# Beginning the second group's 48-point stage inside the first sort, with tile tables by partition

## The chip, the cores and the metric

The kernel runs on one core of a Trainium2 chip. The metric is the device time of one execution in microseconds, as the median of several runs. TensorE (PE in the profile) multiplies matrices into PSUM, VectorE (DVE) and ScalarE (ACT) work on SBUF and PSUM, GpSimd (POOL) works on SBUF and issues the scatters, SyncE (SP) issues most loads and stores.

## The reference

Two layers follow each other. The first is a long convolution: every one of 8 batches of 5696 tokens with 128 channels is convolved with a filter by a real FFT of twice the length. The second is a mixture of 8 experts: each token goes to the expert with the largest logit, through two matrices with a ReLU between, and is scaled by its probability.

```python
Xf = np.fft.rfft(x, n=2 * S, axis=1); Hf = np.fft.rfft(h, n=2 * S, axis=0)
y = np.fft.irfft(Xf * Hf[None], n=2 * S, axis=1)[:, :S]
logits = y.reshape(B * S, D) @ w_gate
expert_idx = np.argmax(logits, axis=1)          # probs = softmax(logits)
out[mask_e] = probs_e * (np.maximum(y[mask_e] @ w1[e], 0) @ w2[e])
```

## The kernel before

The transform is split into 120 points along one axis and 48 along the other. The 8 batches form three groups of 2, 3 and 3. Each group passes three phases. `phase_a` is the 120-point DFT: it reads x, and its results go to a DRAM buffer U. `phase_b` is the 48-point stage: 120 items for the second and third group, each with a forward product (tile xp, read from a load uq of U), a multiplication by the filter (`product`: three VectorE operations into zt and xs, with the filter's tile hh), a sum of the two (`combine`, zt), an inverse product (vp), and a copy (`save`) that goes to DRAM as V. An item's product runs one step after its xp, its sum two, its vp four, its copy five steps after. For the sums `ALONE` says from which item on GpSimd takes them instead of VectorE; for the splits of the third group (`cut`) `FIRST` says so. `phase_c` is the 120-point inverse, the gate and the sort: `score` and `route` find each token's expert, `rank` counts on VectorE where each token goes in a DRAM buffer SR that is sorted by expert (pi), and `sort` scatters the rows there from GpSimd, six a rank, with a small memset between two (`REST`, into a spare `mi` or `hh` buffer). In the first group `lift` brings the 48-point results from the SBUF tile `big` by transposes.

After the sort of a group `tables` computes on one partition, with some thirty-five small VectorE operations, which row and expert each tile of 256 sorted tokens has. `fill` pads SR behind the last token of each expert after the last sort, from ScalarE's DMA queue, with the tile `dummy` as its source. `experts` then takes tile after tile: load xr, weights wb (loaded only where the expert changes), transposes mx, first layer mh, ReLU hs, second layer ma, and a scatter to the output.

The order of all instructions is written out by hand: every phase is a generator that yields a planned cost, and `run` interleaves them by cost over share. Four calls of `run` follow each other: the first group's DFT; its 48-point stage beside the preparation of the weights; its sort beside the second group's DFT (`SHARES[1]`) and the rest of the preparation; and at last the experts beside `rest`, in which the second and third group pass their 48-point stage and sort. There the experts wait until `begin` marks a part as ready. That is when the next group's 48-point stage has been given `HEAD` ns of planned cost; two pieces of `tables` are emitted after each of its steps. Between two of these calls the SBUF pools close and new ones open. SP works off its loads and stores in the order in which they were emitted.

Of the kernel before, what the change touches and what calls it, by code (L numbers as in the profile page):

```python
# [40 lines left out]
FIRST = 12  # L41
# [7 lines left out]
SHARES = (0.42, 0.195, 0, 0.75, 0.998, 0.42)  # L49
GAP = 5000  # L50
AHEAD = 2
ALONE = (0, 14, 10)
# [9 lines left out]
XR = 19  # L62
PACE = (1800, 2200)
ROOM = 28
REST = (224, 288, 288)
# [6 lines left out]
def conv_moe(ctx: ExitStack, tc: tile.TileContext, I, out, B, S, D, E, F, split):  # L72
# [17 lines left out]
    KEEP = ("wb", "hs")  # L90

    class Space:
# [9 lines left out]
        def tile(self, shape, dt, tag, name, **kw):  # L102
            return (keep if tag in KEEP + ("base", "did") else self.pool).tile(shape, dt, tag=tag, name=name, **kw)

# [94 lines left out]
    jrow = load_const("jrow", [1, total])  # L199
# [241 lines left out]
    def phase_b(gr):  # L441
# [126 lines left out]
        def inverse(n):  # L568
# [4 lines left out]
            vp = ps.tile([P, 512], F32, tag="cx", name=f"vp{g}_{q}_{c}", bufs=4)  # L573
# [141 lines left out]
    def phase_c(pt, guest=None):  # L715
# [75 lines left out]
        def settle(n, k):  # L791
            if k == 0:
                tag, bufs = ("rt", 6) if g else (("hs", 4), ("rt", 3))[n % 2]
# [78 lines left out]
        def rank(n):  # L872
# [46 lines left out]
        for n in range(n_end + 1):  # L919
            for k in range(nsub):  # L920
# [37 lines left out]
    def tables(pt):  # L958
# [3 lines left out]
        cnt = sb.tile([1, E], F32, tag="cnt", name=f"cnt{g}")  # L962
        nc.vector.tensor_tensor(out=cnt, in0=base[0:1, :E], in1=base0[0:1, :E], op=ALU.subtract)
        ci = sb.tile([1, E], I32, tag="ci", name=f"ci{g}")
        nc.vector.tensor_scalar(
            out=ci, in0=cnt, scalar1=float(T - 1 if last else 0), scalar2=None, op0=ALU.add
        )
        nc.vector.tensor_scalar(out=ci, in0=ci, scalar1=SHIFT, scalar2=None, op0=ALU.arith_shift_right)
        yield
        nt = sb.tile([1, E], F32, tag="nt", name=f"nt{g}")  # L970
        nc.vector.tensor_copy(nt, ci)
        prior = state.get("done")
        if prior is not None:
            nc.vector.tensor_tensor(out=nt, in0=nt, in1=prior, op=ALU.subtract)
        end = sb.tile([1, E + 1], F32, tag="end", name=f"end{g}")
        none = E if down else 0
        nc.vector.memset(end[:, none : none + 1], 0.0)
        for k in range(E):
            if k % 4 == 0:
                yield  # L980
# [4 lines left out]
        low, high = slice(0, E), slice(1, E + 1)  # L985
        ahead, upto = (end[:, high], end[:, low]) if down else (end[:, low], end[:, high])
        start = sb.tile([1, E + 1], F32, tag="start", name=f"start{g}")
        nc.vector.memset(start, float(E * CAP))
        here, after = (start[:, high], start[:, low]) if down else (start[:, low], start[:, high])
        if prior is not None:  # L990
            nc.vector.tensor_tensor(out=here, in0=prior, in1=ahead, op=ALU.subtract)
        else:
            nc.vector.tensor_scalar(out=here, in0=ahead, scalar1=-1.0, scalar2=None, op0=ALU.mult)
        nc.vector.scalar_tensor_tensor(
            out=here, in0=here, scalar=float(T), in1=base0[0:1, :E], op0=ALU.mult, op1=ALU.add
        )
        stp = sb.tile([1, E], F32, tag="stp", name=f"stp{g}")
        nc.vector.tensor_tensor(out=stp, in0=after, in1=here, op=ALU.subtract)
        jr = jrow[:, :NT]
        yield  # L1000
        ge = sb.tile([1, E, NT], F32, tag="yt", name=f"ge{g}")
        nc.vector.tensor_tensor(
            out=ge,
            in0=jr.rearrange("p (o j) -> p o j", o=1).broadcast_to([1, E, NT]),
            in1=upto.rearrange("p (e o) -> p e o", o=1).broadcast_to([1, E, NT]),
            op=ALU.is_ge,
        )
        yield
        ej = sb.tile([1, NT], F32, tag="ej", name=f"ej{g}", bufs=1)
        nc.vector.tensor_reduce(out=ej, in_=ge.rearrange("p e j -> p j e"), axis=AX.X, op=ALU.add)  # L1010
        yield
        nc.vector.tensor_tensor(
            out=ge, in0=ge, in1=stp.rearrange("p (e o) -> p e o", o=1).broadcast_to([1, E, NT]), op=ALU.mult
        )
        yield
        r0 = sb.tile([1, NT], F32, tag="r0", name=f"r0{g}", bufs=1)
        nc.vector.tensor_reduce(out=r0, in_=ge.rearrange("p e j -> p j e"), axis=AX.X, op=ALU.add)
        yield
        nc.vector.scalar_tensor_tensor(out=r0, in0=jr, scalar=float(T), in1=r0, op0=ALU.mult, op1=ALU.add)
        nc.vector.tensor_scalar(out=r0, in0=r0, scalar1=start[:, none : none + 1], scalar2=None, op0=ALU.add)  # L1020
        tab = const.tile([1, 3, NT], I32, name=f"tab{g}")
        nc.vector.tensor_scalar(out=tab[:, 0, :], in0=r0, scalar1=float(E * CAP), scalar2=None, op0=ALU.min)
        yield
        nc.vector.tensor_scalar(out=ej, in0=ej, scalar1=float(E - 1), scalar2=None, op0=ALU.min)
# [17 lines left out]
        nc.vector.tensor_tensor(out=tab[:, 2, back:], in0=ej[:, back:], in1=ej[:, : NT - back], op=ALU.not_equal)  # L1042
        yield
        pt.need = const.tile([1, 1], I32, name=f"need{g}")
        nc.vector.tensor_copy(pt.need, end[:, E - none : E - none + 1])
        pt.tab = tab
# [3 lines left out]
        if not last:  # L1050
            did = sb.tile([1, E], F32, tag="did", name=f"did{g}")
# [7 lines left out]
            state["done"] = did  # L1059

# [242 lines left out]
    def chain(*gens):  # L1303
        for x in gens:
            yield from x
# [47 lines left out]
    g0 = groups[0]  # L1353
    with tc.manual_schedule():
# [10 lines left out]
        run((chain(*[gather(pt) for pt in g0.parts]), 1.0), (phase_a(groups[1]), SHARES[1]), (prep, SHARES[5]))  # L1365
# [83 lines left out]
```

## Time and profile before

| what | value |
|---|---|
| median of 3 runs | 2157.73 us (2156.82 to 2159.77) |
| the profiled execution | 2157.51 us |
| its span, first to last instruction | 2155.7 us |
| TensorE busy | 2082.7 us, 97% |
| VectorE, ScalarE, GpSimd busy | 1542.5, 1114.9, 1350.0 us |
| mean granted TensorE clock | 0.976 |

The profile is of one execution. Its page cuts the span into 40 slices of 53.9 us and gives for each the busy tenths of the engines and the granted clock of TensorE. Where TensorE is busy at full clock, a slice shows 9 in both lines. The stretches in which it doesn't are looked at in the trace: windows for sums, events in order of time for who waited for whom, the chain of work that ended last, and groups of instructions by line for the mean time of one.

### The profile page before, as it was taken

What the parts mean: (1) busy time and instruction counts of PE and PEld (TensorE: products, weight loads), DVE (VectorE), ACT (ScalarE), POOL (GpSimd) and SP (SyncE); (2) the same over time, 40 slices, a digit from 0 to 9 for tenths busy, and PEclk for the clock granted to TensorE, in tenths of its full rate; (3) what the DMA queues carried; (4) which work ended last, traced back from release to release, by engine and by line L of the source; (5) the groups of instructions that cost most, each with busy time, mean ns of one, the idle gap of its engine ahead of it and who ended that gap; (6) DMA issues with size and microseconds to landing.
All of it is one profiled execution on the core that took longest, in us unless ns stands there. A gap on an engine that the chain in (4) does not pass through costs nothing.

```text
span 2155.7 us, 47101 instructions
## 1 busy us (share of the span) xinstructions
PE 2082.7 (97%) x14452; PEld 1863.3 (86%) x14452; DVE 1542.5 (72%) x3373; ACT 1114.9 (52%) x2317; POOL 1350.0 (63%) x1569
## 2 busy tenths in 40 slices
PE   9999999799999999989999999999999999999998
PEld 7799777377777889878888888999999999999998
DVE  4698677799997777688888887666665555555554
ACT  5677555143334666534555555555544454444544
POOL 6566388545554388888998775288883444443333
PEclk9999999599999999999999999999999999999999
DMA  8899799999997898868878885656533244343331
GB/s 269 263 289 293 227 297 281 256 237 256 248 267 196 232 276 255 245 168 229 204 205 222 216 203 153 159 132 159 141 103 98 87 132 135 129 133 126 123 121 34
DMA packets 216993, 420.33 MB, mean 195 GB/s; under 512 B 32501, under 2 KB 136235, under 8 KB 216740
## 3 DMA queue, kind: packets, MB, share of 16 engines
q1 hardware_dynamic: 187263, 360.52, 59.7%
q0 software_dynamic: 27072, 55.35, 8.9%
q8 instruction: 117, 1.92, 0.4%
q10 hardware_dynamic: 2405, 1.43, 0.2%
q14 instruction: 136, 1.11, 0.2%
HBM read 582.45 MB, written 154.27 MB: 342 GB/s over the span
## 4 chain that ended last, share of the span: by engine, by line
PE 82%; DMA 9%; DVE 3%; POOL 2%; issue 2%; ACT 1%; SPq 1%; ACTq 0%; POOLq 0%; DVEq 0%
PE mh L167 23%; PE ma L167 22%; PE vp L167 9%; PE xp L167 9%; PE yp L167 5%; PE mx L189 4%; PE pa L167 3%; DMA xt<-x 3%; PE gb L167 2%; DMA wb<-WD 2%; DMA mt<-mq 2%; PE tp L189 1%; PE hp L167 1%; PE lb L189 1%; DMA U<-ut 1%
## 5 line engine op out<-in xcount | busy, mean ns | idle before, releaser
L1173 DVE SCALAR_TENSOR_TENSOR hs<-mh,hs 128x512 fp32r<-128x512 f32 x728 | 501.6, 689 | 387.5 <-ACT hs L1171 381.2
L167 PE MATMUL mh<-xtb,wb 128*128 128x256 f32 x4368 | 706.4, 297 | 23.0 <-DVE hs L1173 5.2
L1171 ACT ACTIVATE hs<-mh 128x512 fp32r<-128x512 f32 x728 | 435.4, 598 | 488.1 <-PE mh L167 475.4
L167 PEld LDWEIGHTS mh<-xtb,wb 128*128 128x128 f32 x4368 | 589.8, 191 | 92.6 <-issue 37.9
L167 PE MATMUL ma<-hs,wb 128*128 128x256 f32 x4368 | 658.3, 287 | 1.7 <-DMA wb<-WD 1.7
L167 PEld LDWEIGHTS ma<-hs,wb 128*128 128x128 f32 x4368 | 574.4, 191 | 2.9 <-DMA wb<-WD 2.7
L665 POOL DMA_INDIRECT SR<-rt,pi x384 | 406.0, 1057 | 196.2 <-issue 58.9
L683 POOL DMA_INDIRECT out<-xr x310 | 305.4, 985 | 354.2 <-ACT hs L1171 172.6
L566 POOL TENSOR_TENSOR zt<-zt,xs 128x384 f32<-128x384 f32 (+1 forms) x276 | 295.8, 1074 | 155.2 <-DVE xs L556 103.9
L603 ACT COPY vt<-vp 96x384 f32<-96x384 f32 x240 | 114.2, 476 | 260.8 <-PE vp L167 256.6
L560 DVE TENSOR_TENSOR xs<-xp,hh 64x384 f32<-64x384 f32 (+1 forms) x360 | 214.8, 597 | 7.8
L167 PE MATMUL vp<-zt,mi 128*96 128x384 f32 x480 | 200.5, 500 | 0.0
L551 DVE TENSOR_TENSOR zt<-xp,hh 128x384 f32<-128x384 f32 (+1 forms) x300 | 173.6, 579 | 28.7 <-PE xp L167 18.4
L167 PE MATMUL xp<-uq,mt 96*128 96x384 f32 (+1 forms) x496 | 177.7, 462 | 8.5 <-DMA uq<-U 5.1
L167 PE MATMUL pa<-xc,fcr 120*120 120x512 f32 x576 | 159.4, 411 | 1.9 <-POOL xc L284 1.0
L556 DVE SCALAR_TENSOR_TENSOR xs<-xp,hh 64x384 f32<-64x384 f32 x240 | 134.3, 560 | 4.2
L167 PE MATMUL yp<-vr,gcr 120*120 120x384 f32 x576 | 119.5, 343 | 7.1 <-ACT ut L317 7.1
L167 PEld LDWEIGHTS vp<-zt,mi 128*96 128x96 f32 x480 | 79.7, 167 | 49.8 <-issue 26.7
L167 PEld LDWEIGHTS pa<-xc,fcr 120*120 120x120 f32 x576 | 99.9, 186 | 25.2 <-DVE rk L884 2.6
L167 PEld LDWEIGHTS xp<-uq,mt 96*128 96x128 f32 x496 | 87.6, 200 | 33.5 <-issue 12.8
L317 DVE COPY ut<-pa 120x512 f32<-120x512 f32 x96 | 65.7, 684 | 68.6 <-PE pa L167 54.7
L749 DVE TENSOR_TENSOR vr<-vq,vr 120x768 fp32r<-120x768 f32 x96 | 91.5, 954 | 31.8 <-ACT vr L748 31.0
(165 smaller groups left out, 2720.9 us busy)
## 6 DMA issues: line engine op xcount, KB each, us to landing
wb<-WD SPq DMA_DIRECT2D x728, 512.0 KB
U<-ut SPq DMA_DIRECT2D x48, 720.0 KB
uq<-U SPq DMA_DIRECT2D x60, 576.0 KB
V<-vt SPq DMA_DIRECT2D x60, 576.0 KB
vq<-V SPq DMA_DIRECT2D x48, 720.0 KB
xt<-x SPq DMA_DIRECT2D x96, 240.0 KB
hh<-HS SPq DMA_DIRECT2D x120, 192.0 KB
xr<-SR SPq DMA_DIRECT2D x155, 130.0 KB
```

Of the source, the lines that this page charges most:

```text
L167: nc.tensor.matmul(to, lhs, rhs, **kw)
L189: nc.tensor.transpose(dst, src, ident[:n, :n])
L551: nc.vector.tensor_tensor(out=zt, in0=x3, in1=hv[:, 0].broadcast_to([P, PK, cb, D]), op=ALU.mult)
L556: nc.vector.scalar_tensor_tensor(out=xs[to, 0], in0=x3[at, 0], scalar=-1.0, in1=him[:, 0], op0=ALU.mult, op1=ALU.mult)
L560: nc.vector.tensor_tensor(out=xs[to], in0=x3[at], in1=him, op=ALU.mult)
L566: eng.tensor_tensor(out=zt, in0=zt, in1=xs, op=ALU.add)
L603: done = nc.scalar.copy(outs_[qb][:, k0 : k0 + PK, c * cw : (c + 1) * cw], banks.pop(n)[:K2, :iw].rearrange("p (q x) -> p q x", q=PK),)
L665: s = nc.gpsimd.indirect_dma_start(out=SR[:, :], out_offset=IndirectOffsetOnAxis(ap=pi[:, b : b + 1], axis=0), in_=rt[:, b, :], in_offset= ...
L683: sc = nc.gpsimd.indirect_dma_start(out=out[:, :], out_offset=IndirectOffsetOnAxis(ap=xr[:, s, D + 1 : D + 2].bitcast(I32), axis=0), in_=x ...
L749: nc.vector.tensor_tensor(out=vr[:, 1], in0=src, in1=vr[:, 0].bitcast(F32), op=ALU.subtract)
L1171: done = nc.scalar.activation(hs[:, 0], hp, AF.Relu)
L1173: done = nc.vector.scalar_tensor_tensor(out=hs[:, 1], in0=hp, scalar=0.0, in1=hs[:, 0].bitcast(F32), op0=ALU.max, op1=ALU.subtract)
```

## The change

The sort of the first group is no longer run to its end beside the second group's DFT. `lifting` runs it until its last transposes from `big` are emitted; then the pools close, and the rest of it (five steps and an end) is run from `rest`: the first loads of the second group's 48-point stage, then the remaining sort steps, with two items of the 48-point stage behind each from the third on (`HEADS`). Then the stage goes on as before, with `HEAD` counted from there. Until the first part is ready, vp takes PSUM banks of tag mh. The tiles of the sort that outlive the pools move to the pool `keep`. The first filter loads take the `hh` buffers in another order, the second of them later. `tables` holds an expert per partition (9 partitions) and takes sums over experts by five small matmuls with a constant `tcol`. The memset between scatters writes `dummy` for all groups, 2 x 112 columns instead of 224 or 288. `SHARES[1]` goes from 0.195 to 0.2, `ALONE` from 14 and 10 to 5 and 8, `FIRST` from 12 to 10.

```diff
-FIRST = 12
+FIRST = 10
...
-SHARES = (0.42, 0.195, 0, 0.75, 0.998, 0.42)
+SHARES = (0.42, 0.2, 0, 0.75, 0.998, 0.42)
...
-ALONE = (0, 14, 10)
+ALONE = (0, 5, 8)
...
+HEADS = 2
...
-REST = (224, 288, 288)
+REST = 112
...
-    KEEP = ("wb", "hs")
+    KEEP = ("wb", "hs", "rt", "yt", "lmax", "ls", "ex", "wm", "oh", "sm", "cum", "rk", "pi", "base", "did")
...
+        def load_h(qb):
+            hhs[qb] = hhbufs[(qb + 2) % 3]
+            for k in range(2):
+                nc.sync.dma_start(hhs[qb][k * HP : k * HP + NB, :QB], HS[:, qb * QB : (qb + 1) * QB])
...
-            if g != 0:
-                hhs[qb] = hhbufs[qb % 3]
-                for k in range(2):
-                    nc.sync.dma_start(hhs[qb][k * HP : k * HP + NB, :QB], HS[:, q : q + QB])
             tiles[qb] = (uq, mi)
+            if g != 0 and (g, qb) != (1, 1):
+                load_h(qb)
...
-            vp = ps.tile([P, 512], F32, tag="cx", name=f"vp{g}_{q}_{c}", bufs=4)
+            tag, bufs = ("mh", 2) if g == 1 and not parts[0].ready else ("cx", 4)
+            vp = ps.tile([P, 512], F32, tag=tag, name=f"vp{g}_{q}_{c}", bufs=bufs)
...
+        if g == 1:
+            yield 0
+            load_h(1)
...
                 if n < nu - QUICK:
-                    idle = hhbufs[2].rearrange("p a b d -> p (a b d)") if g else mibufs[3].rearrange("p a x -> p (a x)")
-                    nc.gpsimd.memset(idle[:, : REST[g]], 0.0)
+                    nc.gpsimd.memset(dummy[:, :, :REST], 0.0)
...
+                if g == 0 and at == total_sub - 3:
+                    state["lifted"] = True
...
-        for k in range(E):
-            if k % 4 == 0:
-                yield
-            e = E - 1 - k if down else k
-            a, b = (e + 1, e) if down else (e, e + 1)
-            nc.vector.tensor_tensor(out=end[:, b : b + 1], in0=end[:, a : a + 1], in1=nt[:, e : e + 1], op=ALU.add)
         yield
...
+        mm(bank[:E1, 0:1], tcol[:, 7 + E1 * down : 7 + E1 + E1 * down], nt, start=True, stop=True)
...
-        ge = sb.tile([1, E, NT], F32, tag="yt", name=f"ge{g}")
-        nc.vector.tensor_tensor(
-            out=ge,
-            in0=jr.rearrange("p (o j) -> p o j", o=1).broadcast_to([1, E, NT]),
...
+        begun, ended, over = col("begun", NT), col("ended", NT), col("over", NT)
+        nc.vector.tensor_scalar(out=begun, in0=jr, scalar1=ahead, scalar2=here, op0=ALU.is_ge, op1=ALU.mult)
+        nc.vector.tensor_scalar(out=ended, in0=jr, scalar1=upto, scalar2=here, op0=ALU.is_ge, op1=ALU.mult)
+        nc.vector.tensor_scalar(out=over, in0=jr, scalar1=upto, scalar2=None, op0=ALU.is_ge)
         yield
...
+        mm(bank[:1, :NT], tcol[:, 5:6], begun, start=True, stop=False)
+        mm(bank[:1, :NT], tcol[:, 6:7], ended, start=False, stop=True)
+        mm(bank[:1, 128 : 128 + NT], tcol[:, 5:6], over, start=True, stop=True)
+        mm(bank[:1, 256:257], nt, tcol[:, 1:2], start=True, stop=True)
...
-            bins = phase_b(gr)
-            for n, cost in enumerate(bins):
-                if guest and n == QN * gr.nch - 12:
+            bins = enumerate(phase_b(gr))
+            if gr.g == 1:
+                next(bins)
+                for n, cost in enumerate(first_sort):
+                    yield cost
+                    if n >= HEADS:
+                        for _ in range(2):
+                            yield next(bins)[1]
+            for n, cost in bins:
+                if guest and n == QN * gr.nch - 12 + (gr.g == 1):
                     guest.start()
...
+    first_sort = gather(g0.parts[0])
+
+    def lifting():
+        while "lifted" not in state:
+            yield next(first_sort)
...
-        run((chain(*[gather(pt) for pt in g0.parts]), 1.0), (phase_a(groups[1]), SHARES[1]), (prep, SHARES[5]))
+        run((lifting(), 1.0), (phase_a(groups[1]), SHARES[1]), (prep, SHARES[5]))
```

## Rows read from the trace of the kernel before

**Rows 1.** the page: TensorE clock in tenths of full speed, 40 slices

```profile
PEclk9999999599999999999999999999999999999999
```

**Rows 2.** windows: busy of PE, PEld, DVE, ACT, POOL; clock, DMA share, GB/s

```profile
400.00:420.00 20.00, 16.95 (x24) 6.03 (x24) 19.05 (x47) 2.37 (x5) 8.82 (x10) 0.50 0.95 263
...
440.00:460.00 20.00, 20.00 (x111) 14.64 (x110) 19.36 (x36) 8.09 (x17) 10.89 (x11) 1.00 0.93 232
```

**Rows 3.** events of 377 to 426 us: start, us, engine, line, operation, idle before

```profile
377.84 0.94 PE L167 MATMUL pa<-xc,fcr 120*120 120x512 f32 x3
...
385.26 1.23 SPq L473 DMA_DIRECT2D uq<-U  x1
...
392.43 0.25 DVE L890 TENSOR_REDUCE pi<-rk 120x6 int32<-120x54 f32 x1
...
394.07 5.46 PE L167 MATMUL xp<-uq,mt 96*128 96x384 f32 x8 [2.72 <-DMA uq<-U]
...
396.15 0.56 DVE L551 TENSOR_TENSOR zt<-xp,hh 128x384 f32<-128x384 f32 x1 [2.35 <-DMA hh<-HS]
...
409.72 1.00 POOL L665 DMA_INDIRECT SR<-rt,pi  x1 [0.30 <-issue]
...
412.27 0.18 DVE L1042 TENSOR_TENSOR tab<-ej 1x36 int32<-1x36 f32 x1
...
413.21 1.99 SPq L1134 DMA_DIRECT2D wb<-WD  x4
...
425.12 1.89 PE L167 MATMUL mh<-xtb,wb 128*128 128x256 f32 x6 [0.46 <-ACT xtb L1155]
```

**Rows 4.** chain that ended last, 300 to 470 us: start, us, engine, tile

```profile
427.01 1.28 PE xp L167 x2
...
432.32 0.65 PE xp L167 x2
```

**Rows 5.** groups by line, 373 to 450 us: busy, mean ns, idle before

```profile
L551 DVE TENSOR_TENSOR zt<-xp,hh 128x384 f32<-128x384 f32 x20 | 11.1, 555 | 3.3 <-DMA hh<-HS 2.4 <-PE xp L167 0.6
...
L566 DVE TENSOR_TENSOR zt<-zt,xs 128x384 f32<-128x384 f32 x14 | 7.8, 559 | 0.4
...
L566 POOL TENSOR_TENSOR zt<-zt,xs 128x384 f32<-128x384 f32 x6 | 6.3, 1054 | 33.7 <-DVE xs L556 33.7
...
L896 POOL MEMSET mi<- 128x224 f32 x19 | 5.9, 309 | 0.0
```

**Rows 6.** windows at the start of the third group's 48-point stage

```profile
950.00:960.00 10.00, 6.68 (x33) 5.11 (x32) 9.58 (x25) 2.82 (x6) 8.23 (x11) 0.83 0.43 101
```

**Rows 7.** events of 953 to 954 us

```profile
953.51 0.36 POOL L896 MEMSET hh<- 128x288 f32 x1
...
953.90 0.78 SPq L480 DMA_DIRECT2D hh<-HS  x2
```

**Rows 8.** VectorE's groups by line, 932 to 985 us

```profile
L1010 DVE TENSOR_REDUCE ej<-ge 1x67 f32<-1x536 f32 x1 | 1.1, 1102 | 0.0
...
L1012 DVE TENSOR_TENSOR ge<-ge,stp 1x536 f32<-1x536 f32 x1 | 0.7, 705 | 0.0
...
L983 DVE TENSOR_TENSOR end<-end,nt 1x1 f32<-1x1 f32 x8 | 1.2, 154 | 0.2
...
L1019 DVE SCALAR_TENSOR_TENSOR r<-c_jrow,r 1x67 f32<-1x67 f32 x1 | 0.2, 216 | 0.0
```

**Rows 9.** events of 1591 to 1612 us, behind the last sort

```profile
1591.89 0.26 DVE L890 TENSOR_REDUCE pi<-rk 120x6 int32<-120x54 f32 x1
...
1600.08 0.39 ACTq L1076 DMA_DIRECT2D SR<-dummy  x1
...
1606.99 0.60 ACT L1171 ACTIVATE hs<-mh 128x512 fp32r<-128x512 f32 x1 [3.74 <-DMA sp_zt<-SR]
...
1608.36 1.52 PE L167 MATMUL mh<-xtb,wb 128*128 128x256 f32 x6 [2.26 <-DVE start L988]
...
1611.36 0.37 POOL L896 MEMSET hh<- 128x288 f32 x1
```

More of the change, by code (lines that the diff above doesn't have):

```diff
@@ L102, in tile @@
         def tile(self, shape, dt, tag, name, **kw):
-            return (keep if tag in KEEP + ("base", "did") else self.pool).tile(shape, dt, tag=tag, name=name, **kw)
+            return (keep if tag in KEEP else self.pool).tile(shape, dt, tag=tag, name=name, **kw)
     sb = Space()
@@ L965, in tables @@
+        cnt = col("cnt")
+        nc.vector.tensor_reduce(out=cnt, in_=diag, axis=AX.X, op=ALU.add)
+        yield
         nc.vector.tensor_scalar(
-            out=ci, in0=cnt, scalar1=float(T - 1 if last else 0), scalar2=None, op0=ALU.add
+            out=cnt, in0=cnt, scalar1=tcol[:, 0:1], scalar2=tcol[:, 1:2], op0=ALU.subtract, op1=ALU.mult
         )
+        ci = col("ci", dt=I32)
+        add = tcol[:, 4:5] if last else tcol[:, 2:3]
+        nc.vector.tensor_scalar(out=ci, in0=cnt, scalar1=add, scalar2=None, op0=ALU.add)
@@ L968, in tables @@
+        yield
         nc.vector.tensor_scalar(out=ci, in0=ci, scalar1=SHIFT, scalar2=None, op0=ALU.arith_shift_right)
[L969 to L970 removed]
+        nt = col("nt")
         nc.vector.tensor_copy(nt, ci)
[L972 removed]
         if prior is not None:
             nc.vector.tensor_tensor(out=nt, in0=nt, in1=prior, op=ALU.subtract)
[L975 to L976 removed]
@@ L987, in tables @@
[L987 to L993, printed above, removed]
-        nc.vector.scalar_tensor_tensor(
-            out=here, in0=here, scalar=float(T), in1=base0[0:1, :E], op0=ALU.mult, op1=ALU.add
-        )
@@ new lines, in tables @@
+        bank = ps.tile([P, 512], F32, tag="cx", name=f"ah{g}", bufs=4)
+        mm(bank[:E1, 0:1], tcol[:, 7 + E1 * down : 7 + E1 + E1 * down], nt, start=True, stop=True)
+        yield
+        ahead, upto, here = col("ahead"), col("upto"), col("here")
+        nc.vector.tensor_copy(ahead, bank[:E1, 0:1])
+        yield
+        nc.vector.tensor_tensor(out=upto, in0=ahead, in1=nt, op=ALU.add)
+        nc.vector.scalar_tensor_tensor(
+            out=here, in0=ahead, scalar=float(-T), in1=at, op0=ALU.mult, op1=ALU.add
@@ L1015, in tables @@
+        mm(bank[:1, 256:257], nt, tcol[:, 1:2], start=True, stop=True)
         yield
         r0 = sb.tile([1, NT], F32, tag="r0", name=f"r0{g}", bufs=1)
-        nc.vector.tensor_reduce(out=r0, in_=ge.rearrange("p e j -> p j e"), axis=AX.X, op=ALU.add)
+        ej = sb.tile([1, NT], F32, tag="ej", name=f"ej{g}", bufs=1)
+        nc.vector.scalar_tensor_tensor(
+            out=r0, in0=jr[0:1], scalar=float(T), in1=bank[:1, :NT], op0=ALU.mult, op1=ALU.add
+        )
+        nc.vector.tensor_scalar(
+            out=ej, in0=bank[:1, 128 : 128 + NT], scalar1=float(E - 1), scalar2=None, op0=ALU.min
+        )
@@ L1018, in tables @@
+        pt.need = const.tile([1, 1], I32, name=f"need{g}")
+        nc.vector.tensor_copy(pt.need, bank[:1, 256:257])
         yield
-        nc.vector.scalar_tensor_tensor(out=r0, in0=jr, scalar=float(T), in1=r0, op0=ALU.mult, op1=ALU.add)
-        nc.vector.tensor_scalar(out=r0, in0=r0, scalar1=start[:, none : none + 1], scalar2=None, op0=ALU.add)
         tab = const.tile([1, 3, NT], I32, name=f"tab{g}")
         nc.vector.tensor_scalar(out=tab[:, 0, :], in0=r0, scalar1=float(E * CAP), scalar2=None, op0=ALU.min)
-        yield
@@ L1049, in tables @@
             nc.vector.tensor_copy(state["left"], ej[:, NT - 1 :])
-        if not last:
-            did = sb.tile([1, E], F32, tag="did", name=f"did{g}")
+            did = sb.tile([E1, 1], F32, tag="did", name=f"did{g}")
             nc.vector.tensor_scalar(
@@ L1059, in tables @@
             state["done"] = did
+            state["at"] = const.tile([E1, 1], F32, name=f"at{g}")
+            nc.vector.scalar_tensor_tensor(
+                out=state["at"], in0=did, scalar=float(T), in1=tcol[:, 3:4], op0=ALU.mult, op1=ALU.add
+            )
     def begin(pt):
@@ L1419 @@
     ltri = (m[:, None] < m[None, :]).astype(f32) - 1
-    jrow = np.arange((B * S - E) // T + E)[None, :]
+    jrow = np.tile(np.arange((B * S - E) // T + E)[None, :], (E + 1, 1))
+    e = np.arange(E + 1)
+    own = (e < E) * 1.0
+    far = (1 << 20) * (1 - own)
+    tcol = np.stack([e * (B * S + T) * own, own, far, e * (B * S + T), (T - 1) * own + far, own * 0 + 1, own * 0 - 1], 1)
+    up = (e[:, None] < e[None, :]) * 1.0
+    dn = ((e[:, None] > e[None, :]) | (e[None, :] == E)) * own[:, None]
+    tcol = np.concatenate([tcol, up, dn], 1)
     ins = {
@@ L1439 @@
         "jrow": jrow.astype(f32),
+        "tcol": tcol.astype(f32),
     }
```

38 lines of the change are left out of this document (11 added, 27 removed).

## The prediction

> **What bounds the kernel now.** I read the clock line of the page first [rows 1]: TensorE is busy nearly throughout, and the one slice at half clock is the eighth, 377 to 431 us, where the first sort ends and the second group's 48-point stage begins. So a gain must come from a stretch where TensorE waits or runs slow. Windows come second [rows 2]: at 400 to 420 us it has 24 matmul instructions at a clock of 0.50, at 440 to 460 us 111 at 1.00 with all 20.00 us busy. Third comes the order of events in that stretch [rows 3]: the last DFT product of the second group at 377.84, the load uq that waits for its result issued at 385.26, the last rank (pi) at 392.43, the first xp at 394.07, its product on VectorE at 396.15 (held by hh), GpSimd's last scatter at 409.72, the tile table at 412.27, the weight loads at 413.21, the first expert matmul mh at 425.12. Two more stretches matter because the edit touches their queues: the start of the third group's 48-point stage at 930 to 980 us [rows 6 to 8] and the pad rows behind the last sort at 1600 to 1620 us [rows 9].
>
> **Part 1: the first window.** Gained: eight more items of the 48-point stage are drawn ahead of the experts (two after each of four sort steps), then eight again as before until HEAD is spent. LULL then lets three more pass. So 19 forward products stand ahead of the first mh, not 11. An item costs TensorE one xp and one vp of the same 384 columns, 0.65 us each at full clock [rows 4], and the window 440 to 460 us, like those after it, has no TensorE time left [rows 2]: 8 x 1.30 = 10.4 us is saved **if the first mh is no later than now**. Break-even: mh 10.4 us later, at 435.5.
>
> Lost: the delay of that mh. What comes sooner is the DFT. Its half steps are planned at 279/0.2 = 1395 instead of 1431, so after 71 of them the last product stands ahead of the sort's step 29, not behind it: some 4.5 us, before 373.5. The order of loads on SP is unchanged, so uq, the first xp and the first product move with it: 380.8, 389.6 and 391.7. What comes later is the sort: now the first two xp stand ahead of its last gate product on TensorE, and the first product stands ahead of rank 14 on VectorE. Rank 15 then stands behind five products and four sums. From 391.7 on VectorE alone has: twelve products of three operations, 0.555 us and two like it (12 x 1.67 = 20.0); the five sums that stay with it (5 x 0.559 = 2.8) [rows 5]; 18 small operations of two ranks and a route, about 0.25 each like pi [rows 3] (4.5); 19 small operations of the table at about 0.2 each like the row of L1019 [rows 8] (3.8). Together 31.1: table at 422.8, instead of 412.4. Behind the table 0.8 us to the weight loads and 11.9 to mh, as now [rows 3]: 435.5, just break-even. But a V store and another set of loads now stand ahead of the weights on SP, on DMA that is 0.95 busy [rows 2]. If they are off the path they cost nothing; if the set takes as long as the first one from issue to use it is 8.8 [rows 3]. I take 2, since V and most of that set are issued while VectorE still works on the table. So mh at 437.5, a delay of 12.4 against 10.4: **+2**. The best end is hh landing 3 us sooner yet, mh at 432.5, **-3**; the worst is the whole 8.8, **+9**. The sums from item 5 on go to GpSimd, behind the scatters. These end at about 415 (rank 15 near 407, after five products, four sums and the 18 small operations; then six at 1.0 and 0.30 each [rows 3]), about when TensorE at half clock asks for the first of them: no term of its own, though 2 us if rank 15 slips by as much.
>
> The Trainium skill ("GPSIMD Engine Reference", 4.1 Engine selection) speaks against that move: an elementwise sum belongs on VectorE, GpSimd takes about twice as long. The trace agrees, 1054 ns against 559 [rows 5]. By the page eleven sums would cost 5.4 us more if GpSimd were last; by the rows it idles 33.7 us before six of them [rows 5], so I price the move by what leaves VectorE.
>
> **Part 2: the third group's start.** From 940 to 970 us VectorE is busy 9.6 of each 10 us and TensorE less than 9; one of the three windows is shown [rows 6]. Here every operation taken off VectorE counts. The old table has two reductions at 1.1 us and two wide operations at 0.7 on one partition [rows 8], 3.6 us; the new one has three comparisons of 67 elements and a few columns in their place, six at about 0.2 like L1019, 1.2 us. The chain of eight one-element sums (1.2 us [rows 8]) becomes a matmul that idle TensorE takes. Two sums (0.56 each) and one cut of the same size go to GpSimd, which by then has ended its sort. Saved: 2.4 + 1.2 + 1.7 = 5.3. Besides, SP's hh load at 953.90 stood behind GpSimd's memset of that buffer (ended 953.87) [rows 7], with weight loads queued behind it; the memset goes to another tile now. VectorE was busy meanwhile, so I add only 0.7. **-6**, from 0 (the two new matmuls that wait for VectorE give it back) to -9.
>
> **Part 3: the pad rows.** The memset between two scatters now writes `dummy`, and `fill` sends `dummy` from ScalarE's queue. So its first DMA must wait for the last memset of the last sort, which GpSimd reaches late. That such a write holds a DMA is what rows 7 show; that a DMA held on ScalarE's queue holds the relus behind it is shown at 1606.99, where a relu waited 3.74 us and TensorE lost 2.26 [rows 9]. Now the first pad DMA leaves at 1600.08 and waits for nothing; the last memset is at 1611.36. Shorter memsets (0.31 instead of 0.37 [rows 5, 9]) help little: from the rank at 1591.9 twelve scatters are still to go, 12 x (1.00 + 0.31) = 15.7 and the gaps between them, so the last memset ends between 1608 and 1611.4; I take 1610. ScalarE stands still for 9.9 us. TensorE has about 1.5 us of slack per held relu (3.74 less 2.26), so it loses some 8.4. After a wait it runs at half clock for a while, as at 427 us [rows 4]: 1 to 3 more. If the wait at 1606.99 falls into the longer one, up to 4 come back. **+9**, from +5 to +12; 0 if nothing holds the DMA.
>
> **Nothing else**: GpSimd's shorter memsets in the other sorts free an engine that is late for nobody until 1600; the kept buffers have the same depths; the table's matmuls of one column are under 1 us per table and fall into stretches where TensorE waits.
>
> **Sum** on the profiled execution, 2157.5 us (0.2 below the median): +2 - 6 + 9 = +5, so 2162.5.
>
> **The rivals.** *The pad DMA holds nothing* (the other side, not slower). Decided at one place: whether the first pad DMA leaves at the time of the last sort's rank or behind the last memset. Then +2 - 6 = -4: 2153.5. Against it: rows 7 show just this kind of wait. *The first window pays.* If TensorE, with vp in banks of its own, is dense enough on the sixteen steps, its clock comes back before the experts start: in the trace it works 17 of 20 us at 0.50 [rows 2], and steps of 2 x 1.28 become 2 x 0.65 [rows 4]. Then the six half-clock us behind the first mh (425 to 432, [rows 4]) cost 3 less, and loads at their early end 5 less: -6 instead of +2, total 2154.5. The Trainium skill ("TensorE: Matmul & The Clock Gate", What's actually happening) has it so: throttled is the default and activity releases it. Rows alone speak for and against: VectorE's 31 us, not TensorE, set the table, so a faster clock gives nothing ahead of mh. *Both of these*: 2145.5. *The interleave starves*: the loads queue fully ahead of the weights, +9 instead of +2: 2169.5. *The change doesn't do what it says*: uq still lands only at 394 and eight items wait in front of the sort's end; that is 4.5 us more in part 1, 2167.
>
> **Chances.** Forecast (2159 to 2166) 0.45; pad holds nothing 0.15; first window pays 0.18; both 0.07; starved or not sooner 0.15. 0.2%, 4.3 us, is about what a measurement of this kernel can tell from no change. Of the forecast's 0.45, 0.33 lie above 2162 and 0.12 within; with the starved cases slower gets 0.48. The two middle rivals lie near the lower bound: 0.16 of them within, so same 0.28, and faster 0.24 with "both". The range reaches to 2149 and 2172 and leaves out most of "both" and the worst ends.
>
> **What would show it.** Right: uq issued near 381, a rank near 395 behind a product, mh near 437 with some 19 xp ahead of it; VectorE under 9.6 of 10 near 950, hh not behind a memset; a gap of some 10 us on ScalarE, with TensorE idle, ahead of the first pad DMA. Wrong: a pad DMA that leaves at once, mh before 433, or a half-clock stretch that ends well before the first mh. The forecast falls if the pad wait isn't there or if the first window is worth more than 6 us either way.

## The result, and the profile after

The changed kernel is slower: 2180.47 us median (2173.44 to 2187.07) beside 2157.72 (2154.17 to 2165.36) of the kernel before on the same chip, ratio 1.0101, 95% interval 1.0077 to 1.0125. The forecast was 2162.5 with a range from 2149 to 2172, so the median lies 8 us beyond it. The profiled execution took 2173.44 us with a span of 2171.7, the shortest of its six; 16.0 over the span before, where +5 was forecast. Its clock line (compare rows 1) has the low slice where it was, and one more, at 923 to 977 us:

```profile
PEclk9999999699999999989999999999999999999999
```

Windows of the first stretch and of the third group's start (columns as in rows 2; compare rows 2 and 6), and below them the one window of the kernel before that rows 2 leave out:

```profile
400.00:420.00 20.00, 14.87 (x33) 6.83 (x31) 16.85 (x39) 3.32 (x7) 11.66 (x13) 0.71 0.69 177
420.00:440.00 20.00, 14.78 (x47) 7.34 (x47) 18.14 (x41) 4.06 (x9) 7.99 (x9) 0.89 0.97 283
440.00:460.00 20.00, 20.00 (x96) 13.71 (x94) 18.13 (x33) 7.63 (x17) 8.98 (x9) 0.94 0.98 233
...
950.00:960.00 10.00, 7.71 (x45) 6.15 (x44) 9.69 (x21) 3.30 (x7) 8.17 (x9) 0.89 1.03 257
```

```profile
420.00:440.00 20.00, 18.97 (x69) 11.79 (x68) 18.30 (x35) 5.45 (x12) 1.30 (x1) 0.73 0.93 236
```

The clock comes back sooner (0.71 at 400 to 420 us, 0.50 before), yet TensorE is busy 14.87 of 20 us there, 16.95 before, and 14.78 in the next 20 us, 18.97 before: it waits where it used to run slowly. VectorE is at 9.69 of 10 at 950, no less than before. Events of 377 to 438 us (start, us, engine, line, operation, idle before; compare rows 3):

```profile
377.83 0.34 SPq L480 DMA_DIRECT2D uq<-U  x1
...
385.89 2.90 PE L168 MATMUL xp<-uq,mt 96*128 96x384 f32 x4 [5.59 <-DMA uq<-U]
...
388.26 0.56 DVE L556 TENSOR_TENSOR zt<-xp,hh 128x384 f32<-128x384 f32 x1 [7.81 <-DMA hh<-HS]
...
404.56 0.25 DVE L899 TENSOR_REDUCE pi<-rk 120x6 int32<-120x54 f32 x1
...
412.16 1.00 POOL L674 DMA_INDIRECT SR<-rt,pi  x1 [0.31 <-issue]
413.17 3.86 POOL L571 TENSOR_TENSOR zt<-zt,xs 128x384 f32<-128x384 f32 x4
...
414.24 1.59 PE L168 MATMUL vp<-zt,mi 128*96 128x384 f32 x2 [5.13 <-POOL zt L571]
...
424.87 0.18 DVE L1048 TENSOR_TENSOR tab<-ej 1x36 int32<-1x36 f32 x1
...
426.16 2.94 SPq L1141 DMA_DIRECT2D wb<-WD  x4
...
437.83 1.35 PE L168 MATMUL mh<-xtb,wb 128*128 128x256 f32 x6 [0.46 <-ACT xtb L1162]
```

uq, xp and the first product come 3 to 4 us sooner still than forecast, the last rank (pi) comes 12 us later than before, and the table at 424.87 instead of 412.27. TensorE stands 5.13 us at 414.24 for a sum that GpSimd takes behind the last scatters. Events behind the last sort (compare rows 9):

```profile
1607.85 0.32 POOL L904 MEMSET dummy<- 128x224 f32 x1
1608.20 0.38 ACTq L1083 DMA_DIRECT2D SR<-dummy  x1
...
1608.69 0.60 ACT L1178 ACTIVATE hs<-mh 128x512 fp32r<-128x512 f32 x1 [13.12 <-POOL dummy L904]
...
1610.07 1.65 PE L168 MATMUL mh<-xtb,wb 128*128 128x256 f32 x6 [10.29 <-DVE ci L989]
```

The first pad DMA leaves when the last memset ends; ScalarE has stood 13.12 us, TensorE 10.29. And one place of which the forecast says nothing, a product of the second layer (ma) that waits for weights; the longest wait for weights between 1225 and 1300 us before was 1.32:

```profile
1255.43 1.65 PE L168 MATMUL ma<-hs,wb 128*128 128x256 f32 x6 [3.87 <-DMA wb<-WD]
```

To divide the 16 us I add up TensorE's lost time by stage: over all windows of 10 us, 10 less its busy time times the granted clock, so that a window in which it is busy throughout at full clock loses nothing. The first two rows come from one chip, and so do the next three, rest288_no_inter alone, and the last four (those runs come below); the stages are those of the first trace (us).

| kernel | 0-350 | 350-450 | 450-900 | 900-1050 | 1050-1400 | 1400-1600 | 1600-1750 |
|---|---|---|---|---|---|---|---|
| before | 23.0 | 29.8 | 11.2 | 24.0 | 6.6 | 1.1 | 10.8 |
| after | 19.5 | 33.6 | 12.9 | 20.8 | 12.3 | 2.0 | 19.0 |
| before_again | 25.4 | 28.7 | 16.5 | 25.3 | 7.4 | 3.2 | 11.2 |
| after_again | 21.6 | 35.4 | 24.5 | 31.5 | 14.4 | 14.7 | 25.9 |
| b_rest224 | 21.7 | 29.6 | 19.4 | 26.7 | 5.1 | 20.1 | 26.0 |
| rest288_no_inter | 22.1 | 22.1 | 15.3 | 16.9 | 5.0 | 4.1 | 4.3 |
| after_third | 19.9 | 35.5 | 22.5 | 36.7 | 11.0 | 14.2 | 26.4 |
| mi224 | 26.4 | 35.5 | 23.5 | 32.1 | 14.3 | 12.2 | 18.8 |
| mi288 | 26.3 | 34.4 | 18.5 | 29.3 | 13.1 | 2.9 | 12.8 |
| mi288_no_inter | 31.7 | 22.1 | 11.3 | 24.1 | 4.4 | 3.1 | 10.5 |

Between the first two rows: +3.8 in the first window, +1.7 behind it, -3.2 at the third group's start, +5.7 at 1050 to 1400, +0.9 in the last sort, +8.2 at the pad rows, and -3.5 ahead of 350 us, where next to nothing is changed: 13.6 of the 16.0.

How much a stage varies by itself shows in best_repeat (fifth group), the same kernel as mi288_no_inter on the same chip: it loses 24.9, 23.2, 16.9, 19.6, 4.2, 3.9 and 8.3 in the seven stages. Against 31.7, 22.1, 11.3, 24.1, 4.4, 3.1 and 10.5 that is 7 us apart ahead of 350 and 4 to 6 in the two stages from 450 to 1050, but about 1 in the first window and less from 1050 to 1400.

### The profile page after: what moved, and what is told of

It reads as the page before. It is cut to its first block, busy times and chain, and to the rows that moved or that the text cites. A ratio compares the mean times of both kernels' runs of the same rounds, so it can differ in the third digit from the quotient of the medians.

```text
span 2171.7 us, 47146 instructions
## 1 busy us (share of the span) xinstructions
PE 2075.9 (96%) x14482; PEld 1859.5 (86%) x14482; DVE 1526.1 (70%) x3333; ACT 1114.4 (51%) x2317; POOL 1346.6 (62%) x1581
## 4 chain that ended last, share of the span: by engine, by line
PE 80%; DMA 8%; DVE 4%; POOL 3%; issue 2%; ACT 1%; SPq 1%; ACTq 0%; POOLq 0%; DVEq 0%
PE mh L168 22%; PE ma L168 22%; PE vp L168 7%; PE xp L168 7%; PE yp L168 6%; PE pa L168 5%; PE mx L190 3%; PE gb L168 3%; DMA wb<-WD 2%; PE tp L190 2%; DMA mt<-mq 1%; PE lb L190 1%; DMA xr<-SR 1%; PE hp L168 1%; PE gb_None L168 1%
## 5 line engine op out<-in xcount | busy, mean ns | idle before, releaser
L168 PE MATMUL mh<-xtb,wb 128*128 128x256 f32 x4368 | 705.1, 297 | 28.7 <-DVE ci L989 10.3
L168 PEld LDWEIGHTS ma<-hs,wb 128*128 128x128 f32 x4368 | 573.0, 191 | 11.7 <-DMA wb<-WD 11.3
L571 POOL TENSOR_TENSOR zt<-zt,xs 128x384 f32<-128x384 f32 (+1 forms) x287 | 305.8, 1068 | 140.9 <-DVE xs L561 89.6
L168 PEld LDWEIGHTS pa<-xc,fcr 120*120 120x120 f32 x576 | 99.1, 185 | 24.5 <-DVE rk L893 2.3
L758 DVE TENSOR_TENSOR vr<-vq,vr 120x768 fp32r<-120x768 f32 x96 | 91.6, 956 | 35.5 <-ACT vr L757 35.0
```

Of the source, the lines that this page charges most:

```text
L168: nc.tensor.matmul(to, lhs, rhs, **kw)
L571: eng.tensor_tensor(out=zt, in0=zt, in1=xs, op=ALU.add)
L758: nc.vector.tensor_tensor(out=vr[:, 1], in0=src, in1=vr[:, 0].bitcast(F32), op=ALU.subtract)
```

## The experiments

Every ratio below is to the kernel before, run beside it on the same chip; the chips differ (before took 2186.9, 2170.0, 2155.3, 2167.1 and 2167.3 us in the five groups of runs, of which the last two share a chip).

**First group.** One part of the change undone, or done alone. In own_idle the memset of the last sort alone leaves dummy:

```diff
-                    nc.gpsimd.memset(dummy[:, :, :REST], 0.0)
+                    idle = dummy[:, :, :REST] if g < 2 else hhbufs[2].rearrange("p a b d -> p (a b d)")[:, : 2 * REST]
+                    nc.gpsimd.memset(idle, 0.0)
```

> The changed kernel, but in the last group's sort the memset between two scatters writes a spare filter buffer again and not dummy. Theory (the forecast's third term): the pad DMA then leaves when the last rank is done, near 1600, ScalarE's 13.1 us of waiting ahead of 1608.69 and TensorE's 10.29 us ahead of 1610.07 go, the old waits of about 2.3 us come back: some 8 us less, near 2172. Rival (the wait only takes the place of others that come anyway): within 2 us of the changed kernel, near 2180.

In no_inter the first sort runs to its end, and the 48-point stage begins behind it:

```diff
-        run((lifting(), 1.0), (phase_a(groups[1]), SHARES[1]), (prep, SHARES[5]))
+        run((first_sort, 1.0), (phase_a(groups[1]), SHARES[1]), (prep, SHARES[5]))
...
-                next(bins)
-                for n, cost in enumerate(first_sort):
...
-            tag, bufs = ("mh", 2) if g == 1 and not parts[0].ready else ("cx", 4)
+            tag, bufs = "cx", 4
```

> The changed kernel, but the first sort runs to its end beside the second group's DFT, and the 48-point stage begins behind it, as before the change. Theory (the forecast's first term, read again from the changed kernel's trace as some 3 us): near 2177. Rival (the interleave costs most of the 22 us between the medians, since it also sets where the experts' weight loads and the later stages fall): near 2165. Rival on the other side (the interleave pays and other parts cost): above 2184.

b_dummy is the kernel before with `memset(dummy[:, :, :112], 0.0)`, b_tables the kernel before with the new `tables` and their constants.

> The kernel before, and only the memset between two scatters goes to dummy, 2 x 112 columns, in all groups. Theory: the pad rows' wait alone, +8, less 0.7 for the filter load near 954 that no longer stands behind a memset: near 2165. Rival (nothing held, or cover from the old waits): near 2157.

> The kernel before, and only the tables with an expert per partition (with their five matmuls). Theory (3.6 us of VectorE's work ahead of the third group, of it about 2.4 + 1.2 as forecast): -3, near 2154.5. Rival (the matmuls' waits give it back): within 1 us of 2157.7. Rival (TensorE waits in order for VectorE at each of the two groups of table matmuls): +2 or more, near 2160.

Measured: own_idle 1.0275 (1.0243 to 1.0307), no_inter 1.0157 (1.0115 to 1.0199), b_dummy 1.0219 (1.0185 to 1.0253), b_tables 1.0016 (0.9988 to 1.0044). b_tables gained nothing, against its theory; which of its two rivals holds, the interval does not tell. own_idle and b_dummy missed both of their expectations, and no_inter came out, as a ratio, where its rival on the other side had it. None of the theories had b_dummy 42 us above before: a memset that nobody waits for until 1600 us costs more than the whole change did on the first chip. Since the changed kernel was not run beside them, the time of own_idle alone decides nothing on the pad rows. What b_dummy changes besides the target is the length, 224 columns instead of 288 in two groups.

**Second group.** That length, and both kernels again.

```diff
-REST = (224, 288, 288)
+REST = (224, 224, 224)
```

is b_rest224; rest288 is the changed kernel with the memsets of the later groups at 288 columns of `hhbufs[g]`.

> The kernel before, unchanged, for a trace from the same chip as the runs beside it. Both theories: within 0.3% of its other runs there. If the chip of the experiments so far is the cause of the long times, its trace shows which stretch is longer than in the first trace (2155.7).

> The changed kernel, unchanged, beside the kernel before on this chip. If the chips differ by a constant only, 1.010 of before again. Rival: where the kernel before is longer on a chip, the changed kernel loses more than 1.010 there, since it has less cover for late loads; then 1.015 or above.

> The kernel before, with only the length of the memset changed: 224 columns in all groups instead of 224, 288 and 288, into the same spare buffers as before. Theory (only the target, dummy, matters): as before, within 0.2%. Rival (the length matters): 15 us or more above before, most of what the run with dummy and 224 columns in the kernel before showed (1.022).

> The changed kernel, with the memset between two scatters of the second and third group back at 288 columns of a filter buffer; the first group's stays on dummy at 224. Theory (pad rows' wait alone): as the run with only the last group's memset moved off dummy, some 8 us below the changed kernel. Rival (the shorter memset itself costs, 0.31 us instead of 0.36, since the scatters of the sort crowd something else): clearly lower, by 15 us or more below the changed kernel.

Measured: before_again 0.9993 (0.9975 to 1.0012), after_again 1.0250 (1.0214 to 1.0286), b_rest224 1.0182 (1.0148 to 1.0216), rest288 1.0070 (1.0043 to 1.0098). Both rivals that had the length as a cost came out (b_rest224, rest288). So the length matters, target or no target: the kernel before loses 38 us by 0.05 us less in each of 276 pauses. The windows say where (columns as in rows 2), before_again first, b_rest224 second:

```profile
1400.00:1600.00 200.00, 196.77 (x1570) 192.00 (x1569) 133.89 (x427) 112.53 (x247) 168.96 (x240) 1.00 0.55 138
```

```profile
1400.00:1600.00 200.00, 186.32 (x1420) 179.58 (x1420) 120.17 (x384) 103.15 (x222) 144.36 (x217) 0.97 0.52 129
```

With less memset GpSimd does less in the last sort, not more, and VectorE, ScalarE and TensorE too. What is late is seen at the relus. b_rest224, events of 1467 to 1472 and 1554 to 1558 us:

```profile
1467.48 0.95 PE L167 MATMUL mh<-xtb,wb 128*128 128x256 f32 x6
...
1468.98 0.87 PE L167 MATMUL mh<-xtb,wb 128*128 128x256 f32 x6
1470.98 0.60 ACT L1171 ACTIVATE hs<-mh 128x512 fp32r<-128x512 f32 x1 [3.94 <-PE ma L167]
...
1555.91 0.87 PE L167 MATMUL mh<-xtb,wb 128*128 128x256 f32 x6
...
1557.25 0.07 SPq L1134 DMA_DIRECT2D wb<-WD  x1
1557.31 0.60 ACT L1171 ACTIVATE hs<-mh 128x512 fp32r<-128x512 f32 x1 [5.10 <-PE mh L167]
```

and before_again:

```profile
1575.86 0.95 PE L167 MATMUL mh<-xtb,wb 128*128 128x256 f32 x6
...
1576.91 0.60 ACT L1171 ACTIVATE hs<-mh 128x512 fp32r<-128x512 f32 x1 [2.37 <-PE mh L167]
```

In before_again the relu starts as its matmul ends (1576.81, 1576.91). In b_rest224 ScalarE is idle and the matmuls of the relu at 1470.98, those of 1467.48, ended at 1468.43 by the profile: 2.55 us late. At 1557.25 a weight load of SyncE, which waits for TensorE as well, leaves together with the late relu. Counting relus of 1400 to 1600 us that start over 0.5 us behind both the end of their matmuls and ScalarE's instruction before: 16 of 64 in b_rest224, 14 of 65 in after_again, 15 of 66 in b_dummy; 2 of 71 in before_again and 2 of 72 in rest288; none in the first traces of before (73) and after (72), though that after has 224 columns too. So the chip takes part in it. The last sort takes 260 us from its first scatter to its last instead of 236; that the late relus, by the matmuls that they hold, make up these 24 us is an inference.

What is late there is TensorE's signal, by the trace's own record of the signals. In both first traces and in those of the third group, every recorded signal of TensorE but two stands within 0.06 us of the end of an instruction that gives it. In the traces of the other groups 116 to 250 do not (131 of 2040 in before_again, 214 of 2084 in b_rest224), while VectorE's, ScalarE's and GpSimd's do there too, but for two of each engine. The one ahead of the relu at 1470.98 is recorded at 1470.90. Late signals go with GpSimd's scatters. Of the signals with at most one scatter started in the 5 us ahead of them, 0 of 1083 are late in before_again and 1 of 1115 in b_rest224; of those with three or more, 125 of 447 and 207 of 446. Between 1400 and 1600 us that makes 16 of 134 and 56 of 144. Why scatters in close succession go with a late signal, and on some chips alone, is not shown. Matmul ends are modelled, and in these traces some 15% of TensorE's signals are missing (2040 of 2399 recorded in before_again, all but one in the first trace), so that a releaser named there is less sure. The length is not all of it either: b_tables, with 288 columns on the slowest of the chips, has 49 of 142 late between 1400 and 1600 us.

**Third group.** The length further up, and the other parts without the short memset.

```diff
-REST = (224, 288, 288)
+REST = (224, 352, 352)
```

is b_rest352, rest352 the same in the changed kernel; rest288_no_inter joins rest288 and no_inter; rest288_alone_back is rest288 with `ALONE = (0, 14, 10)` and `FIRST = 12`.

> The changed kernel with the memset between two scatters of the second and third group at 352 columns of a filter buffer. Theory (what the shorter memset took away was room between two scatters, and 288 columns are about enough): within 0.4% of the same kernel at 288, 1.003 to 1.011 of before. Rival (every column more helps, the 288 were short as well): below 1.003 of before. Rival on the other side (GpSimd is late for the last sort by 144 times 0.06 us more, 9 us): 1.011 or above.

> The kernel before with the memset of the second and third group at 352 columns instead of 288. Theory (288 are enough): within 0.3% of before. Rival (every column more helps): 0.995 or less. Rival on the other side (GpSimd's time is what the last sort waits for): 1.004 or more.

> The changed kernel with the memset at 288 columns of a filter buffer and without the interleave (the first sort runs to its end beside the second group's DFT, then the 48-point stage). What is left of the change: tables, sums and cuts sooner on GpSimd, SHARES[1] 0.2, kept tiles, the filter order. Theory (what remains of the loss, 1.007, comes from the first window and the later stages that shift with it): 0.999 to 1.003 of before. Rival (it comes from the sums on GpSimd or from the tables): 1.005 to 1.010.

> The changed kernel with the memset at 288 columns of a filter buffer and with ALONE (0, 14, 10) and FIRST 12 as before, so that VectorE keeps its sums as long as before. Theory (the sums on GpSimd stand behind the scatters of rank 15: vp waited 5.1 us for zt in the first window): 1.003 to 1.005 of before, 5 us less than with the sums moved. Rival (VectorE's chain is then longer by nine sums of 0.56, which costs what it saves): 1.006 to 1.009.

Measured: rest352 1.0113 (1.0075 to 1.0152), b_rest352 1.0041 (1.0016 to 1.0065), rest288_no_inter 0.9952 (0.9935 to 0.9969), rest288_alone_back 1.0104 (1.0062 to 1.0146). Longer than 288 is worse again, by 8 us in the kernel before; 138 pauses of the last sort that are 0.05 us longer each come to 7 us of GpSimd's time, an estimate that fits, though the cause is not shown. Taking the sums back does not help, against its theory. Without the interleave the rest of the change is faster than before, and faster than its theory had it. Events of rest288_no_inter at 380 to 418 us show what the interleave displaces:

```profile
380.78 0.64 SPq L480 DMA_DIRECT2D uq<-U  x1
...
389.73 0.25 DVE L899 TENSOR_REDUCE pi<-rk 120x6 int32<-120x54 f32 x1
...
391.08 0.56 DVE L556 TENSOR_TENSOR zt<-xp,hh 128x384 f32<-128x384 f32 x1
...
398.98 0.18 DVE L1049 TENSOR_TENSOR tab<-ej 1x36 int32<-1x36 f32 x1
...
402.83 3.30 SPq L1142 DMA_DIRECT2D wb<-WD  x4
...
409.42 1.00 POOL L674 DMA_INDIRECT SR<-rt,pi  x1 [0.30 <-issue]
...
414.77 2.61 SPq L1114 DMA_DIRECT2D xr<-SR  x3
...
418.06 1.90 PE L168 MATMUL mh<-xtb,wb 128*128 128x256 f32 x6 [0.46 <-ACT xtb L1163]
```

The last rank (389.73) stands ahead of the first product (391.08), the table is ready at 398.98 and the weights are asked for at 402.83, both ahead of the last scatter (409.42); what mh waits for is then the sorted rows, loaded at 414.77, and it comes at 418.06: 19.8 us sooner than with the interleave, 7 sooner than before. The start of this stretch moves by 10 us and more from trace to trace. Taken from the last rank to the first mh, it is 28.3 us here, 24.9 to 25.9 in the other kernels without the interleave, 28.4 in b_tables, 32 to 34 in the kernels with the old tables, and 33 to 35 with the interleave, where the last rank itself comes at 405 to 414 us, not at 390 to 404.

**Fourth group.** A chain on one chip; each kernel from mi224 on differs from the one above it in one thing. In what was expected, a is the interleave, b the wait of the pad rows and c the length of the memset.

after_third is the changed kernel. 

> The changed kernel, unchanged, as the first link of a chain on one chip. 1.010 of before if the chip is like the first and the fourth call's, 1.025 if it is like the third's.

mi224 moves the target only:

```diff
-                    nc.gpsimd.memset(dummy[:, :, :REST], 0.0)
+                    idle = (dummy[:, :, :REST], mibufs[3].rearrange("p a x -> p (a x)")[:, :224], hhbufs[2].rearrange("p a b d -> p (a b d)")[:, :224])[g]
+                    nc.gpsimd.memset(idle, 0.0)
```

> The changed kernel with the memset of the second group in a spare mi buffer and that of the third in a filter buffer, 224 columns as in the changed kernel. Theory (b is the pad rows' wait, 8 us in the first profile): 0.003 to 0.005 below the changed kernel. Rival (waits of the same length come in its place): within 0.001.

mi288 has 288 in place of both 224. 

> As the run before it in this chain, but 288 columns. Theory (c matters only on chips whose traces show late relus in the last sort): within 0.002 of the 224 columns on a chip like the first, 0.015 below them on one like the third call's. Rival (c matters everywhere): 0.005 or more below on any chip.

mi288_no_inter is mi288 without the interleave. 

> As the run before it in this chain, but without the interleave. Theory (a is most of the loss: TensorE lost 17 us more between 350 and 450 with it, and its first expert matmul came 20 to 28 us later): 0.007 to 0.012 below it, 0.993 to 0.996 of before. Rival (the earlier run without it gained from the memset's place, 9 us): 0.003 below it, at about 1.000 of before.

| kernel | median us | to before | step |
|---|---|---|---|
| before | 2167.12 | 1 | |
| after_third | 2226.26 | 1.0279 (1.0249 to 1.0310) | |
| mi224 | 2222.31 | 1.0250 (1.0214 to 1.0286) | target: 4 us |
| mi288 | 2181.40 | 1.0058 (1.0040 to 1.0077) | length: 41 us |
| mi288_no_inter | 2154.16 | 0.9940 (0.9915 to 0.9965) | interleave: 27 us |

What is left against before is 13 us of gain. The target's 4 us are seen at the pad rows, after_third first, mi224 second:

```profile
1654.04 0.38 ACTq L1083 DMA_DIRECT2D SR<-dummy  x1
1654.53 0.60 ACT L1178 ACTIVATE hs<-mh 128x512 fp32r<-128x512 f32 x1 [12.43 <-POOL dummy L904]
1655.91 1.65 PE L168 MATMUL mh<-xtb,wb 128*128 128x256 f32 x6 [7.66 <-DVE ci L989]
```

```profile
1649.44 0.39 ACTq L1084 DMA_DIRECT2D SR<-dummy  x1
...
1664.56 1.65 PE L168 MATMUL mh<-xtb,wb 128*128 128x256 f32 x6 [3.45 <-issue]
```

In after_third the first pad DMA leaves 10.1 us behind the last rank, when the last memset ends, in mi224 2.1 us behind it with 8.6 us of memsets and scatters still to come; TensorE's longest wait there is 7.66 and 3.45 us, 4.2 apart. The late relus between 1400 and 1600 us go with the length, 9 of 67 and 7 of 68 with 224 columns, 2 of 71 and 3 of 72 with 288.

By stages (table above) the interleave loses 12.3 in the first window and 8.7 from 1050 to 1400, both far beyond what the repeat shows. The 7.2 to 900 and 5.2 to 1050 are not: the kernel without it loses 16.9 and 19.6 there when it is run again. mi288's long stalls:

```profile
960.00 0.19 PE L168 MATMUL rj<-c_tcol,nt 9*1 9x1 f32 x2
...
960.87 0.81 PE L168 MATMUL vp<-zt,mi 128*96 128x384 f32 x2
...
970.26 0.21 DVE L1021 SCALAR_TENSOR_TENSOR r<-c_jrow,rj 1x67 f32<-1x67 f32 x1 [7.49 <-remote]
...
971.72 0.47 ACT L609 COPY vt<-vp 96x384 f32<-96x384 f32 x1 [10.89 <-remote]
...
972.25 1.59 PE L168 MATMUL vp<-zt,mi 128*96 128x384 f32 x2 [8.50 <-ACT vt L609]
```

```profile
1185.35 0.96 PE L168 MATMUL mh<-xtb,wb 128*128 128x256 f32 x6 [2.85 <-DMA wb<-WD]
1278.29 0.98 PE L168 MATMUL ma<-hs,wb 128*128 128x256 f32 x6 [3.57 <-DMA wb<-WD]
```

mi288_no_inter has one stall over a microsecond at 1150 to 1300:

```profile
1160.29 0.95 PE L168 MATMUL mh<-xtb,wb 128*128 128x256 f32 x6 [1.31 <-DMA wb<-WD]
```

The stall at 972 us is again a late signal, not the interleave's order: VectorE and ScalarE take up rj and vp 10 us behind the ends of their matmuls (960.19 and 961.68), each within 0.1 us of a recorded signal of TensorE (970.24 and 971.65). Every interleaved kernel traced, with any length, has a second-layer product that waits 2.4 to 4.3 us for weights between 1255 and 1295 us; in the others the longest wait for weights from 1225 to 1300 us is 1.58, on a first-layer product. This loss is the interleave's on every chip. How the shift of the experts against the 48-point stage brings these loads late was not tried.

**Fifth group.** mi288_no_inter again, and with the sums and cuts taken back (ALONE, FIRST as before):

> The changed kernel without the interleave, memset at 288 columns in a spare mi and a filter buffer, again, beside the run with the sums taken back. 0.993 to 0.996 of before.

> As the run beside it, with ALONE (0, 14, 10) and FIRST 12 as before. Theory (the tables carry the gain: in the first window their last piece came at 399 instead of 412, and the first expert matmul at 418 instead of 425): 0.993 to 0.997 of before, within 0.001 of the run beside it. Rival (the sums carry it, since nine sums of 0.56 us leave VectorE just there): 0.998 or more.

Measured 0.9956 (0.9939 to 0.9973) and 0.9957 (0.9931 to 0.9983), as the theory had it. The earlier sums on GpSimd are worth nothing, so the gain is with the tables and what stayed with them (SHARES[1], kept tiles, filter order, the memset's tile); which of these was not separated. b_tables, tables alone in the kernel before, shows the window 350 to 450 at 23.9 us lost instead of 28 to 30, but its whole time was not shorter on its chip. Either of these two kernels beats both.

## Why the prediction was right or wrong

**The step that failed** is the one that put everything outside three stretches at nothing ("Nothing else"). In the first trace the three terms came to +3.8 - 3.2 + 8.2 = 8.8 us for a forecast of +5. The largest of the rest is +5.7 from 1050 to 1400 us, where the interleave makes a second-layer product wait for weights, and no term stood for it. The other part put at nothing, the length of the memset, was worth 41 us where it was run apart, on another chip. How much of the result's 23 us it is on the first chip stays open.

**The first window's schedule** held: first xp before 390, a rank behind a product, 19 items ahead of the first mh, mh at 437.83 (437.5 forecast). Two errors cancelled: the chain began 3.4 us sooner (product at 388.26, not 391.7) and took 36.6 us to the table, not 31.1; the 2 us for loads ahead of the weights did not come. The loss there was +3.8, +2 forecast, inside its bounds. The exclusion of a term for GpSimd's sums failed (5.13 us at 414.24).

**What the term was set against** was the first error. It compared with the kernel before and so counted eight items as saved. Without the interleave the rest of the change brings the first mh from 32.7 us behind the last rank (33.3 in before_again) to 24.9 to 28.3; the interleave takes that away. The tables alone (b_tables) make it 28.4; what the rest comes from is not shown. The interleave's price is 12 us in the window against the change without it (34.4 and 22.1), not 2.

**Where the stall goes next** is the second error. The first window's term ended with the first mh, and what the later start of the experts does behind it was not asked. The interleaved kernels lose again from 1050 to 1400, 8.7 us in the fourth group and 5.7 in the first trace. From 450 to 1050 the figures (7.2 and 5.2; +1.7 and -3.2) are within what a stage varies by itself.

**The third group's start**: -3.2, -6 forecast, in a stage that varies by some 5 us from run to run, so neither is confirmed. The filter load no longer waits for a memset, as foreseen. VectorE stayed at 9.69 of 10, and the 1.7 us for sums and cuts were worth nothing (fifth group).

**The pad rows**: the wait is there as described, first pad DMA at 1608.20, ScalarE 13.12 us, TensorE 10.29; +8.2 in the first trace for a forecast of +9. As a step of the chain it was 4 us; the intervals of the two ratios overlap, and the trace's 4.2 us there agree. Why less of it is left on that chip is not shown.

**"Nothing else"**, more closely: "GpSimd's shorter memsets ... free an engine that is late for nobody" took the pause for dead time. On two chips its length was worth 41 us (fourth group) and 38 (b_rest224 beside before), more than all that the forecast summed. For the first chip it was not run apart; the parts otherwise come to about the 23 us measured there (27 + 8 - 13 = 22, an estimate, since 27 and -13 are from another chip), and its trace has neither a late relu nor a late signal of TensorE. Both speak for a small cost there; it was not measured.

**The rivals.** That the pad DMA holds nothing fell. "The first window pays" was right on the clock (0.71 and 0.89 instead of 0.50 and 0.73 in the two windows) and wrong on what it is worth, as the sentence against it said: VectorE sets the table. The section cited there of the Trainium skill ("TensorE: Matmul & The Clock Gate", What's actually happening) says that activity releases the clock. The first of the two windows agrees, with 33 matmul instructions at 0.71 beside 24 at 0.50; the second has the higher clock with fewer (47 at 0.89, 69 at 0.73), so these rows alone do not show it. The other one ("GPSIMD Engine Reference", 4.1 Engine selection, of the Trainium skill) speaks against elementwise sums on GpSimd: without the interleave they neither cost nor gain (0.9956 with them, 0.9957 without).

**The range** was too narrow: it had bounds for its three terms and none for the parts that were called free, and the medians stand 7 us further apart than the profiled executions, which one trace can't tell.

## What to carry to other kernels

Set each part of a change against the change without that part, not only against the kernel before: a part that nearly breaks even may eat what another gains. Follow a later start on through the stages behind it, and treat the length of a filler (here the memset between two scatters) as a tuned size until a run shows that it isn't. A tile that a DMA reads as its source is a poor place for a filler's writes.

## What the runs showed of the hardware

A memset of 224 instead of 288 columns between two scatters (0.31 and 0.36 us) made the last sort 24 us longer on one chip and was not seen in a profile on another; relus started up to 3.2 us behind the modelled end of their matmuls. On the chips of the first, second, fourth and fifth groups 116 to 250 of TensorE's some 2000 recorded signals come more than 0.06 us behind the end of any instruction that gives one, nearly all of them behind two or more of GpSimd's scatters within 5 us; on those of the first two traces and the third group only two do, and the signals of VectorE, ScalarE and GpSimd are on time on all. A DMA on ScalarE's queue whose source had a memset to come held ScalarE's own work for 13.12 us. Chips differ in more than a factor: the same two kernels stood at 1.010, 1.025 and 1.028 to each other on three chips, with before at 2157.7, 2170.0 and 2167.1 us.
